# A linear-attention and MLP block on one core: a head with fewer constant matmuls, a written ScalarE order, and four row norms on GpSimd

## The chip, the cores and the metric

The kernel runs on one core of a Trainium2 chip. A core has a matrix engine (TensorE, PE in the profile, with its weight loads as PEld), a vector engine (VectorE, DVE), a scalar engine (ScalarE, ACT), GpSimd (POOL) and SyncE (SP), which here only issues DMAs. The metric is the device time of one execution in microseconds; lower is better.

## The reference

`x` is 1 x 2048 x 448 in bfloat16. It is normalised row by row (mean and variance over the 448 columns, no scale or shift), and two branches read the result.

```
xn = layernorm(x)
q, k, v = split(xn @ wqkv)            # 16 heads of 28
pq, pk = phi(q), phi(k)               # phi(t) = t + 1 where t > 0, else exp(t); + 1e-6
kv = sum_s pk[s] v[s]^T ;  z = sum_s pk[s]        # per head
s  = ((pq @ kv) / (pq . z + 1e-6)) @ wo
h  = relu(xn @ w1 + b1)^2             # 1792 columns
g  = silu(h @ w2 + b2)
out = x + s * g
```

## The kernel before

**Tiles.** The 2048 rows are 16 tiles of 128 rows (`si`), in four groups of four (`g`). The 448 columns are contracted in chunks of 128, 128, 128 and 64; the last 64 columns use half the array, so the kernel pairs two matmuls on the two halves. The 1792 hidden columns are 14 slots (`fi`). Results go through eight PSUM banks.

**A planner sets the order.** The program is first a list of operations. `add` (L54) records one: its engine, what it reads and writes, and a duration that the author wrote down. TensorE and SyncE keep the order of the program text. For ScalarE, VectorE and GpSimd, `one_pass` (L98) plays the list through with those written durations and picks, whenever an engine is free, the most urgent ready operation by its due time or by a fixed `prio`; some operations may float between ScalarE and VectorE. It also hands out the banks. `behind` holds an operation until another has been placed, and `at` overrides when the planner believes a DMA lands. The chip then runs each engine's list strictly in that order, with semaphores for the dependences. So a changed duration or landing time can move operations that the edit does not name.

**The head, tiles 0 to 3.** For each tile: two statistics instructions on VectorE (`bn`, `ag`, L490 and L491), ln and exp on ScalarE for the reciprocal deviation (`ln`, `rs`, L498 and L502), the norm on VectorE (`xn`, L520), transposes on TensorE (`T`, L597), and their evacuation to `xT` (`eT`, L606 and L607, most on ScalarE). The last 64 columns of a pair of tiles are copied beside themselves by a twin copy (`tw`, L536 or L537), transposed together (`TR`, L621) and evacuated (`eTR`, L631). TensorE then does the K projection of tiles 0 and 1 (`K0`, `K1`, L795) and two hidden slots (`Ha0`, `Ha1`, L823, on tiles 0 and 1 as `.0` and on tiles 2 and 3 as `.2`), with a small transpose of the bias between them (`B1`, L1228). Ahead of and between these stand matmuls on a zeroed tile `dum` (`warm`, L1213): 30 at once, 9 that wait for the statistics of tile 0, and 6 between T0 and T1.

**The body.** TensorE goes through the hidden slots of group 0 in pairs (`H0.2` to `H0.13`, L780), then `K2|K3`, then the second MLP product (`G`, L1086) of tiles 0 to 3, each `G` in parts over the slots: G0|G1, G2|G3, then the second half of G0|G1, which reads the squares of the later slots, and so on. Then it takes up group 1 with `H1.0`. Each `H` result is a bank that ScalarE or VectorE turns into `relu` (`re`, L758 or L755), and two slots at a time are squared (`sq`, L770 or L769). Each `K` is turned into phi by an exp on ScalarE (`ex`, L701) and a min and a max on VectorE (`mi`, L706, and `ma`, L713); the max frees the bank.

**Tiles 4 to 7** do not go through TensorE's transpose. Their norms are written interleaved, two tiles alternating by column (`xn_cols`); VectorE copies the twins (`tw4`, `tw6`) and transposes 32 x 32 blocks as 32-bit words into `stage` (`tr4`, `tr6`, L557), and 16 DMAs (13 issued by SyncE, 3 by ScalarE, each of 32 KB) put the blocks into `xT`. H1.0 waits for all of them. Tiles 8 to 15 follow the same way later, with `gbuf` in the place of `stage`.

**GpSimd** writes masks and constants until 7.3 us (L371 to L415) and, when w_q has landed, one small scaled copy (`wqh`, L1278). Before the kernel's own code the framework writes four small constants on GpSimd (L1380 in the profile), among them a bfloat16 1.0.

Of the kernel before, what the change touches and what calls it, by code (L numbers as in the profile page):

```python
# [9 lines left out]
P = 128  # L10
# [12 lines left out]
SWAP = 1  # L23
# [23 lines left out]
class Program:  # L47
# [6 lines left out]
    def add(self, eng, emit, reads=(), writes=(), dur=0.2, alts=(), nbytes=0, mode=None, label="", slow=1.0):  # L54
        op = Op(eng, emit, reads, writes, dur, alts, nbytes, mode, label)
        op.slow, op.behind, op.at = slow, None, None
        for t in op.reads:
            op.raw.add(self.writer[t])
            self.readers.setdefault(t, []).append(op)
        for t in op.writes:  # L60
            w = self.writer.get(t)
            if w is not None and w is not op:
                op.deps.add(w)
            for r in self.readers.get(t, ()):
                if r is not op:
                    op.deps.add(r)
            self.writer[t] = op
            self.readers[t] = [r for r in self.readers.get(t, ()) if r is op]
        op.raw.discard(op)
        op.deps |= op.raw  # L70
        for d in op.deps:
            d.succ.append(op)
        self.ops.append(op)
        return op
# [233 lines left out]
def bass_recurrent_scan__linear_attn_block__dense_activation_squared_relu__prompt_kernel(  # L308
    nc, A_x, A_wqkv, A_wo, B_x, B_w1, B_b1, B_w2, B_b2, out
):  # L310
    with ExitStack() as es:
        sb = lambda name, shape, dtype: es.enter_context(nc.sbuf_tensor(name, shape, dtype))
        bf, f32 = dt.bfloat16, dt.float32
        pr = Program()
        add = pr.add

        ident = sb("ident", [P, P], bf)
        dum = sb("dum", [P, P], bf)
# [8 lines left out]
        xn = sb("xn", [P, NT, 512], bf)  # L327
# [8 lines left out]
        b1r = sb("b1r", [NF, P], bf)  # L336
        b1f = sb("b1f", [P, NF], f32)
        b2b = sb("b2b", [P, D], bf)
        st6 = sb("st6", [P, NT, 6], f32)
        mv = sb("mv", [P, NT, 2], f32)  # L340
        vep = sb("vep", [P, NT], f32)
        rstd = sb("rstd", [P, NT], f32)
# [18 lines left out]
        ps = lambda b: pbank[b.bank]  # L361
# [124 lines left out]
        def hp(si, k):  # L486
            return None if si > 3 else 5 * si + k - 25
# [18 lines left out]
        def xn_cols(si, lo, hi):  # L506
            if si < 4 * SWAP:
                return xn[:, si, lo:hi]
            pair_of = xn[:, si // 2 * 2 : si // 2 * 2 + 2, :].rearrange("p t f -> p (t f)")
            return pair_of.rearrange("p (f t) -> p f t", t=2)[:, lo:hi, si % 2]  # L510
# [4 lines left out]
            return v.rearrange("p (j k t) -> p j k t", j=2, t=2)[:, si % 4 // 2, :, si % 2]  # L515

        def ln_norm(si):
            add(
                "dve",
                lambda e, _: e.tensor_scalar(  # L520
                    out=xn_cols(si, 0, D), in0=x_tok[:, si, :], scalar1=mv[:, si, 0:1],
                    scalar2=rstd[:, si : si + 1], op0=ALU.subtract, op1=ALU.mult,
                ),
                [("x", si), ("mv", si), ("rstd", si)], [("xn", si)], 0.39 if si < 4 * SWAP else 0.54, label=f"xn{si}",
            ).prio = hp(si, 3)

        def ln_twin(lo, hi):
# [61 lines left out]
        def pe_transpose(si, pieces):  # L589
            for lo, hi, eng in pieces:  # L590
                b = Buf("T")

                def f(e, _, lo=lo, hi=hi, b=b):
                    v = ps(b)[:, :].bitcast(bf)
                    last = None
                    for c in range(lo, hi):
                        last = e.transpose(v[:, (c - lo) * P : (c - lo + 1) * P], xn[:, si, c * P : (c + 1) * P], ident[:, :])  # L597
                    return last

                add("pe", f, [("xn", si), "ident"], [b], 0.0558 * (hi - lo), mode="128", label=f"T{si}.{lo}")  # L600

                def ev(e, eng, lo=lo, hi=hi, b=b):
                    src = ps(b)[:, 0 : 64 * (hi - lo)].bitcast(bf)
                    dst = xT[:, si, lo:hi, :].rearrange("p c k -> p (c k)")
                    if eng == "dve":
                        return e.tensor_copy(dst, src)  # L606
                    return e.activation(out=dst, in_=src, func=AF.Copy)  # L607

                n = hi - lo
                add(  # L610
                    eng, ev, [b], [("xT", si, c) for c in range(lo, hi)],
                    0.15 + 0.07 * n if eng == "dve" else 0.18 + 0.107 * n, label=f"eT{si}.{lo}",
                ).prio = -30
# [590 lines left out]
            return b, reads, mm, out_, D, f"S{si}", 4  # L1204


        def warm(n, after=()):
            b = Buf("W")

            def f(e, _):  # L1210
                last = None
                for _i in range(n):
                    last = e.matmul(ps(b)[:, 0:P], dum[:, 0:P], dum[:, 0:P], start=True, stop=True)  # L1213
                return last

            add("pe", f, ["dum", *after], [b], n * 0.075, mode="128", label="warm")

        for i in range(4):
            ln_stats(i)
            ln_rstd(i, i + 1)  # L1220
            ln_norm(i)
            if i % 2:
                ln_twin(i - 1, i + 1)

        def bias_cols():
# [4 lines left out]
            )  # L1230
            add("act", lambda e, _: e.activation(out=b1f[:, :], in_=ps(bb)[:, 0 : NF // 2].bitcast(bf), func=AF.Copy), [bb], ["b1f"], 0.2, label="b1f")

        warm(30)
        warm(9, [("mv", 0)])
        pe_transpose(0, ((0, 3, "act"),))
        warm(6)
        pe_transpose(1, ((0, 3, "act"),))
        k_part(0, 0, 3)
        pe_transpose_rests(0)
        k_part(1, 0, 3)  # L1240
        head_part(0, 0)
        pe_transpose(2, ((0, 3, "act"),))
        head_part(0, 1)
        bias_cols()
# [4 lines left out]
        head_part(2, 1)  # L1249
        head_rest(0)  # L1250

        order = "bn0 ag0 bn1 ag1 xn0 xn1 bn2 ag2 bn3 ag3 xn2 xn3".split()
        byname = {op.label: op for op in pr.ops}
        for a, b in zip(order, order[1:]):
            byname[b].behind = byname[a]
            byname[b].prio = -25 + order.index(b)
        landing = {("x", 0): 2.9, ("x", 1): 3.55, ("x", 2): 4.7, ("wk", 0): 5.8, ("wk", 3): 5.0, ("wk", 4): 5.4, ("w10", 0): 7.0, ("w10", 3): 7.2, ("w10", 4): 7.4, ("b1r", None): 7.6, ("w11", 0): 9.7, ("w11", 3): 10.0, ("w11", 4): 10.3, ("x", 4): 11.4}
        for (name, k), t in landing.items():
            byname["dma" + str((name, k) if k is not None else name)].at = t

        def ln(lo, hi):
            for si in range(lo, hi):
                ln_stats(si)
            ln_rstd(lo, hi)
            for si in range(lo, hi):
                ln_norm(si)
            ln_twin(lo, hi)
# [86 lines left out]
        a, b = "G10|G11", "G12|G13"  # L1354
# [40 lines left out]
```

## Time and profile before

| | us |
|---|---|
| median of 3 runs | 143.94 (143.91 to 144.25) |
| the profiled execution | 143.42 |
| its span, first to last instruction | 142.2 |
| TensorE busy | 138.6 |
| VectorE busy | 103.2 |
| ScalarE busy | 78.9 |
| GpSimd busy | 6.2 |

Times in the profile run from the start of the span. The 1.2 us between the span and the execution's time lie outside the instructions, and the median of the runs is 0.52 us above the profiled execution. A row of the timeline has start, length, engine, line, operation, output and inputs, count, and in brackets the engine's idle time ahead of it with what ended it. A row of the chain has start, length, engine and line of the work that led to the end.

### The profile page before, as it was taken

The numbers are of one execution on the slowest core, as the hardware profiler recorded it, in microseconds if no ns is written. First come the engines' busy times: TensorE is split into PE (matmuls) and PEld (weight loads), VectorE is DVE, ScalarE is ACT, GpSimd is POOL, SyncE is SP. The second block draws the span as 40 slices with busy tenths as digits, with TensorE's granted clock in tenths as the row PEclk, the third lists the DMA queues.
The fourth block names the chain that finished last, engine by engine and source line by source line (L and its number), as shares of the span: only waits on it lengthen the run. The fifth ranks groups of instructions, "written<-read, shape, count | busy, mean of one in ns | idle before, by whom it ended". The sixth has DMA issues, their size and how long they took to land.

```text
span 142.2 us, 3235 instructions
## 1 busy us (share of the span) xinstructions
PE 138.6 (97%) x1300; PEld 71.7 (50%) x1300; DVE 103.2 (73%) x222; ACT 78.9 (55%) x146; POOL 6.2 (4%) x40
## 2 busy tenths in 40 slices
PE   7999999999999999999999999999999999999992
PEld 7954445454444544444544444445547455555472
DVE  2847999689498899769787799786035516874875
ACT  3578898040888724997863757797139430301412
POOL 7900000000000000000000000000000000000000
PEclk9999999999999999999999999999999999999999
DMA  4999994238933000232000000000697000223033
GB/s 97 319 306 311 344 271 72 34 53 254 227 44 55 14 0 0 46 53 44 9 5 0 0 0 5 0 0 19 156 214 155 1 0 22 93 83 101 32 97 97
DMA packets 23500, 12.91 MB, mean 91 GB/s; under 512 B 14274, under 2 KB 22718, under 8 KB 23486
## 3 DMA queue, kind: packets, MB, share of 16 engines
q1 hardware_dynamic: 21550, 11.24, 31.5%
q10 hardware_dynamic: 1936, 1.48, 4.3%
q8 instruction: 10, 0.16, 0.5%
q14 instruction: 4, 0.03, 0.1%
HBM read 9.23 MB, written 1.90 MB: 78 GB/s over the span
## 4 chain that ended last, share of the span: by engine, by line
PE 97%; DVE 2%; issue 0%
PE pb L780 29%; PE pb L1086 22%; PE pb L1178 7%; PE pb L881 7%; PE pb L723 7%; PE pb L733 6%; PE pb L1103 4%; PE pb L1213 4%; PE pb L1143 3%; PE pb L860 1%; DVE gbuf L1167 1%; PE pb L887 1%; PE pb L823 1%; PE pb L795 1%; PE pb L1030 1%; PE pb L597 1%
## 5 line engine op out<-in xcount | busy, mean ns | idle before, releaser
L780 PE MATMUL pb<-xT,w 64*128 64x512 bf16 x378 | 43.6, 376 | 0.0
L1086 PE MATMUL pb<-w,r 64*128 64x448 bf16 x336 | 34.6, 349 | 0.0
L758 ACT ACTIVATE r<-pb,b1f 128x512 bf16<-128x512 f32 x40 | 25.7, 686 | 12.9 <-PE pb L780 12.4
L780 PEld LDWEIGHTS pb<-xT,w 64*128 64x128 bf16 x378 | 18.4, 94 | 21.7
L1086 PEld LDWEIGHTS pb<-w,r 64*128 64x128 bf16 x336 | 16.3, 94 | 15.9 <-issue 0.4
L770 ACT ACTIVATE r<-r 128x1024 bf16<-128x1024 bf16 x15 | 15.7, 1062 | 0.6 <-DVE r L755 0.5
L755 DVE TENSOR_SCALAR r<-pb,b1f 128x512 bf16<-128x512 f32 x16 | 11.7, 744 | 4.5 <-PE pb L780 4.5
L1198 DVE TENSOR_TENSOR gbuf<-pb,gbuf 128x448 bf16<-128x448 f32 x14 | 8.1, 618 | 6.6 <-PE pb L1178 6.6
L490 DVE BATCH_NORM_STATS2 st<-x_tok 128x6 f32<-128x448 bf16 x16 | 9.5, 615 | 2.9 <-DMA x_tok<-in_A_x_dram 2.9
L723 PE MATMUL pb<-w_k,xT 64*128 64x448 bf16 x98 | 11.6, 349 | 0.0
L733 PE MATMUL pb<-xT,w_q 64*128 64x512 bf16 x84 | 11.0, 376 | 0.0
L1126 ACT ACTIVATE gbuf<-gbuf 128x448 bf16<-128x448 bf16 x14 | 7.0, 570 | 6.7 <-DVE gbuf L1076 5.9
L1178 PE MATMUL pb<-w_k,pqT 64*128 64x448 bf16 x96 | 10.6, 349 | 0.0
L1076 DVE TENSOR_TENSOR gbuf<-pb,b2b 128x448 bf16<-128x448 f32 x14 | 8.0, 614 | 3.4 <-PE pb L1086 2.0
L713 DVE SCALAR_TENSOR_TENSOR pk<-pb,pk 128x448 bf16<-128x448 f32 x16 | 9.5, 617 | 0.2
L994 DVE TENSOR_TENSOR pqT<-pqT,xT 128x2048 bf16<-128x2048 bf16 x3 | 3.7, 1221 | 8.2 <-DMA xT<-scr 8.2
L701 ACT ACTIVATE pqT<-pb 128x512 bf16<-128x512 f32 x12 | 6.5, 597 | 5.6 <-PE pb L733 5.6
L881 PE MATMUL pb<-pk,xn 128*128 128x448 bf16 x48 | 9.6, 353 | 0.0
L701 ACT ACTIVATE pk<-pb 128x448 bf16<-128x448 f32 x16 | 7.8, 543 | 3.1 <-PE pb L723 2.5
L769 DVE TENSOR_TENSOR r<-r 128x1024 bf16<-128x1024 bf16 x13 | 8.5, 682 | 0.1
L917 DVE TENSOR_TENSOR zacc<-zacc,pk 128x448 f32<-128x448 f32 x13 | 8.0, 618 | 0.1
L520 DVE TENSOR_SCALAR xn<-x_tok,mv,rstd 128x448 bf16<-128x448 bf16 x16 | 7.4, 498 | 0.8 <-ACT rstd L502 0.7
(98 smaller groups left out, 134.6 us busy)
## 6 DMA issues: line engine op xcount, KB each, us to landing
w<-in_B_w_dram SPq DMA_DIRECT2D x1, 1568.0 KB, 10.3
out_dram<-gbuf SPq DMA_DIRECT2D x13, 112.0 KB, 1.7
x_tok<-in_A_x_dram SPq DMA_DIRECT2D x3, 448.0 KB, 5.7
xT<-gbuf SPq DMA_DIRECT2D x32, 32.0 KB, 2.0
w<-in_B_w_dram SPq DMA_DIRECT2D x2, 384.0 KB, 5.9
xT<-scr SPq DMA_DIRECT2D x6, 112.0 KB
w<-in_B_w_dram SPq DMA_DIRECT2D x1, 576.0 KB, 5.5
xT<-scr ACTq DMA_DIRECT2D x5, 112.0 KB
```

The source lines that it names most:

```text
L490: add("dve", lambda e, _: e.bn_stats(st6[:, si, :], x_tok[:, si, :]), [("x", si)], [("st", si)], 0.61, label=f"bn{si}").prio = hp(si, 0)
L701: "act", lambda e, _: e.activation(out=slot, in_=ps(buf)[0:rows, 0:n], func=AF.Exp), [buf, "actw"],
L713: lambda e, _: e.scalar_tensor_tensor(out=slot, in0=ps(buf)[0:rows, 0:n], scalar=1.0 + 1e-6, in1=slot, op0=ALU.add, op1=ALU.max),
L723: return e.matmul(ps(b)[:, 0:D], x_tile(rows, si, c), w_k[rows, c, :], start=start, stop=stop)
L733: return e.matmul(ps(b)[:, 0:512], w_q[rows, c, m * P : (m + 1) * P], x_group(rows, g, c), start=start, stop=stop,)
L755: return e.tensor_scalar(out=slot, in0=ps(b)[:, 0:512], scalar1=b1f[:, fi : fi + 1], scalar2=0.0, op0=ALU.add, op1=ALU.max)
L758: return e.activation(out=slot, in_=ps(b)[:, 0:512], func=AF.Relu, bias=b1f[:, fi : fi + 1])
L770: return e.activation(out=both, in_=both, func=AF.Square)
L780: return e.matmul(ps(b)[:, 0:512], w_1[rows, c, fi * P : (fi + 1) * P], x_group(rows, g, c), start=start, stop=stop,)
L881: last = e.matmul(ps(b)[:, 0:D], xn_cols(si, c * P, (c + 1) * P), pk[:, si, :], start=(si == 0), stop=(si == NT - 1),)
L1086: return e.matmul(ps(b)[:, 0:D], r_cols(rows, fi, si), w_2[rows, fi, :], start=start, stop=stop)
L1178: return e.matmul(ps(b)[:, 0:D], w, msb[rows, c, :], start=start, stop=stop)
```

## The change

Four edits, and what follows from them:

- `warm` can take an operand of its own and then waits for nothing. Three warm-up matmuls on the framework's constant 1.0, seen as a 128 x 128 tile, are put first; of those on `dum`, 9 become 8 and 6 become 3. The planner is told 0.107 us for each instead of 0.075, and for the transposes of tiles 0 and 1 0.107 instead of 0.0558.
- The order of ScalarE's work in the head is written out and held with `behind` and `prio`, as VectorE's already was.
- The norms of tiles 4 to 7 go to GpSimd, with 0.85 us written for each.
- The landing times that the planner is told (`landing`, set through `at`) are replaced.
- The plan that comes out differs in places that no edit names: VectorE and ScalarE trade some relus and squares in groups 0 to 2, the banks are numbered otherwise, and tw4 and tw6 wait for GpSimd. SyncE's list is the same, and so are the lists of all engines from the denominators to the end.

```diff
         def ln_norm(si):
+            by_pool = 4 <= si < 8
             add(
-                "dve",
+                "pool" if by_pool else "dve",
...
-                [("x", si), ("mv", si), ("rstd", si)], [("xn", si)], 0.39 if si < 4 * SWAP else 0.54, label=f"xn{si}",
+                [("x", si), ("mv", si), ("rstd", si)], [("xn", si)], 0.39 if si < 4 * SWAP else 0.85 if by_pool else 0.54, label=f"xn{si}",
             ).prio = hp(si, 3)
...
-                add("pe", f, [("xn", si), "ident"], [b], 0.0558 * (hi - lo), mode="128", label=f"T{si}.{lo}")
+                add("pe", f, [("xn", si), "ident"], [b], (0.107 if si < 2 else 0.0558) * (hi - lo), mode="128", label=f"T{si}.{lo}")
...
-        def warm(n, after=()):
+        one = nc.const_aps.tensor(1.0, [P, P], bf)
+
+        def warm(n, after=(), src=None):
             b = Buf("W")
...
-                    last = e.matmul(ps(b)[:, 0:P], dum[:, 0:P], dum[:, 0:P], start=True, stop=True)
+                    last = e.matmul(ps(b)[:, 0:P], src or dum[:, 0:P], src or dum[:, 0:P], start=True, stop=True)
                 return last
 
-            add("pe", f, ["dum", *after], [b], n * 0.075, mode="128", label="warm")
+            add("pe", f, ["dum", *after] if src is None else [], [b], n * 0.107, mode="128", label="warm")
...
+        warm(3, src=one)
         warm(30)
-        warm(9, [("mv", 0)])
+        warm(8, [("mv", 0)])
         pe_transpose(0, ((0, 3, "act"),))
-        warm(6)
+        warm(3)
         pe_transpose(1, ((0, 3, "act"),))
...
-        order = "bn0 ag0 bn1 ag1 xn0 xn1 bn2 ag2 bn3 ag3 xn2 xn3".split()
         byname = {op.label: op for op in pr.ops}
-        for a, b in zip(order, order[1:]):
-            byname[b].behind = byname[a]
-            byname[b].prio = -25 + order.index(b)
...
+        for first, order in (
+            (-26, "bn0 ag0 bn1 ag1 xn0 xn1 bn2 ag2 bn3 ag3 xn2 xn3"),
+            (-61, "rs1 eT0.0 tw0 eT1.0 ln2 rs2 ln3 rs3 eTR0 eT2.0 b1f"),
+        ):
+            names = order.split()
+            for i, (a, b) in enumerate(zip(names, names[1:])):
+                byname[b].behind = byname[a]
+                byname[b].prio = first + 1 + i
+            if first < -26:
+                byname[names[0]].prio = first
```

More of the change, by code (lines that the diff above doesn't have):

```diff
@@ L1250, in bass_recurrent_scan__linear_attn_block__dense_activation_squared_relu__prompt_kernel @@
         head_rest(0)
-        order = "bn0 ag0 bn1 ag1 xn0 xn1 bn2 ag2 bn3 ag3 xn2 xn3".split()
         byname = {op.label: op for op in pr.ops}
-        for a, b in zip(order, order[1:]):
-            byname[b].behind = byname[a]
-            byname[b].prio = -25 + order.index(b)
-        landing = {("x", 0): 2.9, ("x", 1): 3.55, ("x", 2): 4.7, ("wk", 0): 5.8, ("wk", 3): 5.0, ("wk", 4): 5.4, ("w10", 0): 7.0, ("w10", 3): 7.2, ("w10", 4): 7.4, ("b1r", None): 7.6, ("w11", 0): 9.7, ("w11", 3): 10.0, ("w11", 4): 10.3, ("x", 4): 11.4}
+        for first, order in (
[8 more added lines that the diff above has]
+                byname[names[0]].prio = first
+        landing = {("x", 0): 2.92, ("x", 1): 3.9, ("x", 2): 4.65, ("wk", 0): 5.7, ("wk", 3): 5.7, ("wk", 4): 7.2, ("w10", 0): 6.97, ("w10", 3): 7.2, ("w10", 4): 7.4, ("b1r", None): 7.5, ("w11", 0): 9.1, ("w11", 3): 9.4, ("w11", 4): 9.8, ("x", 4): 11.3}
         for (name, k), t in landing.items():
```

## The prediction

> **What bounds the kernel now.** I read the page's busy shares, then the chain of waits in order of time, then the timeline of the first 36 us, then the GpSimd groups.
>
> ```profile
> PE 138.6 (97%) x1300; PEld 71.7 (50%) x1300; DVE 103.2 (73%) x222; ACT 78.9 (55%) x146; POOL 6.2 (4%) x40
> ...
> PE 97%; DVE 2%; issue 0%
> ```
>
> TensorE holds 97% of the chain, so the rest of the kernel matters only where TensorE waits for it. The chain shows where that can be:
>
> ```profile
> 1.06 4.34 PE pb L1213 x39
> 5.40 0.32 PE pb L597 x3
> 5.72 0.64 PE pb L1213 x6
> 6.36 0.32 PE pb L597 x3
> 6.68 0.84 PE pb L795 x3
> 7.63 0.57 PE pb L795 x3
> ...
> 11.11 9.06 PE pb L780 x84
> ...
> 22.82 2.65 PE pb L1086 x28
> ```
>
> From 11.11 on the steps run at one pace: 84 matmuls of 512 columns in 9.06 us are 0.216 us a pair, 28 of 448 columns in 2.65 us are 0.189 us a pair, and the same shapes cost the same up to the tail. There is nothing to win there, only something to lose. The first 11 us are different: six warm-up matmuls take 0.64 us (0.107 us each), the transposes also 0.107 us each, and three K matmuls first take 0.84 us and then 0.57 us. So the array runs at about half pace until roughly 7.1 us, although the page's PEclk row shows 9 throughout; I take the pace from the spacing.
>
> The timeline gives the waits around the change:
>
> ```profile
> 5.76 0.49 ACT L607 ACTIVATE xT<-pb 128x384 bf16<-128x384 bf16 x1 [0.39 <-PE pb L597]
> ...
> 8.12 0.22 PEld L823 LDWEIGHTS pb<-xT,w 128*128 128x128 bf16 x3 [0.37 <-DMA w<-in_B_w_dram]
> ...
> 9.95 0.55 PEld L823 LDWEIGHTS pb<-xT,w 128*128 128x128 bf16 x6 [0.31 <-DVE xT L606]
> ...
> 12.44 1.15 DVE L490 BATCH_NORM_STATS2 st<-x_tok 128x6 f32<-128x448 bf16 x2 [0.80 <-DMA x_tok<-in_A_x_dram]
> ...
> 19.21 0.96 DVE L520 TENSOR_SCALAR xn<-x_tok,mv,rstd 128x448 bf16<-128x448 bf16 x2
> ...
> 20.44 0.71 DVE L557 STREAM_TRANSPOSE stage<-xn 128x512 f32<-128x512 f32 x1
> 21.07 0.71 DVE L755 TENSOR_SCALAR r<-pb,b1f 128x512 bf16<-128x512 f32 x1
> 21.18 9.76 SPq L429 DMA_DIRECT2D xT<-stage  x13
> ...
> 22.66 2.81 PE L1086 MATMUL pb<-w,r 64*128 64x448 bf16 x28
> ...
> 33.25 0.29 PEld L780 LDWEIGHTS pb<-xT,w 64*128 64x128 bf16 x4
> ```
>
> At 8.12 the first w_1 matmul (Ha0.0) waits for its weights from HBM, not for work that the change shortens. At 9.95 Ha0.2 waits for VectorE's evacuation eT3. The rows from 19.21 to 21.18 are the chain that prepares tiles 4 to 7: norms, twin copy, transpose (tr6), 13 DMAs on SyncE's queue. The last two are its consumers: at 22.66 G2|G3, then G0|G1's second half, and at 33.25 the first weights of H1.0.
>
> ```profile
> L397 POOL TENSOR_SCALAR_AFFINE_SELECT zmask<-zmask 128x32 f32<-128x32 f32 x12 | 2.2, 216 | 0.0
> L373 POOL TENSOR_SCALAR_AFFINE_SELECT ident<-ident 128x128 bf16<-128x128 bf16 x1 | 0.3, 292 | 0.2 <-POOL eps L379 0.2
> L1278 POOL TENSOR_SCALAR wqh<-w_q 128x64 bf16<-128x64 bf16 x1 | 0.2, 242 | 14.2 <-DMA w_q<-in_A_wqkv_dram 14.2
> ```
>
> GpSimd has one TENSOR_SCALAR, of 64 columns, and is otherwise idle after 7.3 us.
>
> **The constant matmuls.** The first three need no `dum`, whose memset ends at 1.00 us, so TensorE can begin near 0.85 (ScalarE's first instruction starts at 0.80) instead of 1.06: -0.21. Ahead of T0 stand 41 instead of 39: +0.21. T0 stays at 5.2. Behind it stand 3 instead of 6: 3 x 0.107 = -0.32. T1 would start at 5.83 instead of 6.15, but xn1 ends at 5.41 + 0.40 = 5.81, so near 5.87. K0 then waits for eT0, which ends at 5.76 + 0.49 = 6.25: it starts near 6.33 instead of 6.47, so 0.14 is left. Half pace lasts for 0.14 us more of K0's work, which gives back about 0.07. K1 ended at 8.03 (7.46 plus three times 0.19); it would end at 7.96, and Ha0.0 still starts at 8.12 when its weights land. In this execution the gain is 0; if the weights land 0.3 us earlier it is up to 0.19. I take 0.05, near the end that the row shows.
>
> **ScalarE's written order.** In the changed program ScalarE's first 25 instructions, through rs4, stand as before; the list pins those of the head. With T1 earlier, eT1 ends 0.25 earlier, and with it ln2, rs2 and xn2 (7.66, which waited 0.38 for rstd). T2 reads xn2 but stands behind Ha0.0 on TensorE, and T3, eT3 and Ha0.2 stand behind those: 0.
>
> **Norms 4 to 7.** VectorE loses four norms at about 0.48 us spacing (0.96 a pair). That hides behind TensorE: 0. GpSimd gets them behind the last constants (done at 7.3) and ahead of wqh, which needs w_q at 21.4 anyway. What is new is that VectorE's twin copies tw4 and tw6 wait for GpSimd. The new plan puts behind tw6: tr6, all three last squares of group 0 (one was on ScalarE), the statistics of tile 8, and K2/K3's phi. SyncE's 13 DMAs wait for tr6, and the second half of G0|G1 on TensorE waits for the squares.
>
> I add up starts on VectorE by the rows' spacing: statistics of 4 and 5 at 12.44 (x lands); +1.29; K1's min and max +0.85 (now behind the statistics); two relus +0.66 each; square +0.61; statistics of 6 and 7 +1.28: 17.79. ScalarE: square 4.5 waits for relu 0.4 until 15.98, +1.0, two relus +0.57 each, ln and exp +0.53: rstd 6 at 18.7. GpSimd runs xn6 and xn7 from 18.75 to 18.75 + 2p. VectorE is free for tw6 at about 20.1.
>
> The price p of one norm, from both sides: from 32 to 128 columns the select goes from 216 to 292 ns, 0.79 ns a column, so wqh's 242 + 384 x 0.79 = 0.55 us at 448. If all of wqh's 242 ns grew with the columns, it would be 242 x 448/64 = 1.69 us. VectorE's own norm goes from 0.40 to 0.53 where the output is interleaved; that ratio on 0.55 gives 0.74. I take 0.74: the slope is GpSimd's own, and the output here is interleaved. Then tw6 starts at 20.3, tr6 ends at 21.24 (before: 21.15), and the third square ends 2.73 us after tw6, at 23.0. G0|G1's second half starts at 22.66 + 14 x 0.0946 = 23.98 and loads weights about 0.15 sooner: 0.8 us of cover. The last staged DMA landed at about 32.3 (issued 30.33, 2.0 to land); H1.0 loads weights at 33.25: 0.9 us of cover. Both are used up at p = 1.15. Below that the cost is 0.
>
> **Another new wait.** H0.8 takes the bank that K1's max frees. That ends now at 12.44 + 1.29 + 0.31 + 0.59 = 14.63 instead of 14.32, and TensorE reaches it at about 14.65: 0 here, and at most 0.1 when the head runs early. It also ties TensorE to x of tile 4 at 12.42, so a gain over 0.1 in the head is lost again here unless that lands earlier too.
>
> **The sum.** The tail's orders are unchanged. 143.42 us (span 142.2 and 1.2 around it) - 0.05 = 143.37. The median of the runs is 0.52 above that execution; I carry the offset: 143.94 - 0.05 = 143.89, rounded to 143.9.
>
> **Rivals.** (1) GpSimd becomes the bound, slower: p over 1.15, and each further 0.1 costs 0.2 us on G0|G1, since two norms stand in series. At 1.5 that is +0.70 (144.6), at the bound of 1.69 +1.08 (145.0). For it: no row has GpSimd at 448 columns, an interleaved output or per-partition scalars. Against it: wqh, the same operation, lies on the line of the other GpSimd rows. VectorE's square 6.7 (18.62 to 19.3) also falls on xn6. In the rows ten selects ran in 1.80 us from 4.41, 0.18 each, across VectorE's xn0 and xn1, so sharing cost little. [...]
>
> (2) The clock, faster: pace doubles near 7.1, 6.0 us after the first matmul. If an earlier start moves that ahead of 6.1, K0 and K1 take 0.57 each from 6.1 and Ha0.0 could start at 7.4 instead of 8.12: up to 0.7 us (143.2) if the w_1 weights are there, 0 if they land at 8.1. [...]
>
> **Chances.** Forecast, all hidden, 143.7 to 144.0: 0.57. GpSimd slow enough to show (p over about 1.4), 0.25. Clock and weights both early, 0.18. A measurement of this kernel can tell about 0.3% (0.43 us) from no change. Range 143.4 to 144.6: it takes in p up to 1.5 and the smaller half of the clock's gain, and leaves out about 0.1 on each side. Faster 0.18, same 0.57, slower 0.25.
>
> **What would show it.** Right: Ha0.0 still waiting for DMA near 8.1; GpSimd's four norms under 1.1 us each; VectorE idle little before tw6; the first L1086 group in one pace. Wrong: a gap in TensorE near 24 or 33 released by VectorE or by DMA, or the first K matmuls already at 0.19 us spacing.

## The result, and the profile after

The changed kernel takes 145.14 us (median of 7 runs, 144.33 to 145.37) against 143.97 for the kernel before on the same chip (143.47 to 144.25): a ratio of 1.0066 with a 95% interval of 1.0038 to 1.0093. It is slower, by 0.7%, and by what the first rival described. The profiled execution took 144.82 us with a span of 143.6, 1.4 longer than the span before.

On the page the three lines to compare are the busy times, the shares of the chain and a group that was not there before.

```profile
PE 138.7 (97%) x1299; PEld 71.4 (50%) x1299; DVE 103.6 (72%) x221; ACT 75.9 (53%) x143; POOL 14.0 (10%) x44
...
PE 80%; DVE 6%; DMA 4%; SPq 4%; POOL 3%; ACT 2%; issue 1%
...
L521 POOL TENSOR_SCALAR xn<-x_tok,mv,rstd 128x448 bf16<-128x448 bf16 x4 | 7.9, 1993 | 7.5 <-ACT rstd L502 7.5
```

TensorE is as busy as before, but it holds 80% of the chain instead of 97%: the chain now runs through other engines for a fifth of the time. The last line has the reason: one GpSimd norm takes 1993 ns, where the forecast took 740 and thought 1690 the most it could be.

The chain shows where that meets TensorE (start, length, what):

```profile
18.33 0.21 ACT rstd L502
...
18.63 3.94 POOL xn L521 x2
...
22.59 0.21 DVE xn L537
...
22.83 0.71 DVE stage L558
23.54 1.79 DVE r L770 x3
...
25.37 1.50 PE pb L1087 x14
```

Read downwards it is the path that the prediction followed: reciprocal deviations of tiles 6 and 7, their two norms in series, the twin copy tw6, the transpose tr6, the three squares, and then G0|G1's second half on TensorE. The weight loads of that half say how long TensorE stood (idle time ahead, and its releaser):

```profile
25.37 1.06 PEld L1087 LDWEIGHTS pb<-w,r 64*128 64x128 bf16 x14 [1.78 <-DVE r L770]
```

These loads run ahead of their matmuls (at G2|G3 they began at 22.35 and the matmuls at 22.54); by the spacing of the matmuls themselves the gap is 1.51 us, and it is the only long one that the trace before does not have. Up to K0 the head went as forecast: T1 starts at 5.79 instead of 6.15 and K0 at 6.26 instead of 6.47, and then

```profile
8.01 0.50 PE L824 MATMUL pb<-xT,w 128*128 128x256 bf16 x3 [0.18 <-DMA w<-in_B_w_dram]
```

the first w_1 matmul still waits for its weights from HBM, which landed 0.11 us earlier in this execution than in the one before. 1.51 - 0.11 = 1.40 is the difference of the spans.

### The profile page after: what moved, and what is told of

Same layout as the page of the kernel before. It is cut to its first block, busy times and chain, and to the rows that moved or that the text cites. A ratio compares the mean times of both kernels' runs of the same rounds, so it can differ in the third digit from the quotient of the medians.

```text
span 143.6 us, 3234 instructions
## 1 busy us (share of the span) xinstructions
PE 138.7 (97%) x1299; PEld 71.4 (50%) x1299; DVE 103.6 (72%) x221; ACT 75.9 (53%) x143; POOL 14.0 (10%) x44
## 4 chain that ended last, share of the span: by engine, by line
PE 80%; DVE 6%; DMA 4%; SPq 4%; POOL 3%; ACT 2%; issue 1%
PE pb L781 22%; PE pb L1087 20%; PE pb L1179 7%; PE pb L882 6%; PE pb L734 6%; PE pb L724 6%; DMA x_tok<-in_A_x_dram 4%; SPq L429 4%; PE pb L1104 4%; PE pb L1144 3%; POOL xn L521 3%; PE pb L861 1%; DVE r L770 1%; DVE gbuf L1168 1%; PE pb L888 1%; PE pb L1031 1%
## 5 line engine op out<-in xcount | busy, mean ns | idle before, releaser
L1087 PE MATMUL pb<-w,r 64*128 64x448 bf16 x336 | 34.7, 349 | 1.3 <-DVE r L770 1.3
L1087 PEld LDWEIGHTS pb<-w,r 64*128 64x128 bf16 x336 | 16.2, 94 | 17.5 <-DVE r L770 1.8
L771 ACT ACTIVATE r<-r 128x1024 bf16<-128x1024 bf16 x12 | 12.6, 1059 | 0.5 <-DVE r L756 0.4
L770 DVE TENSOR_TENSOR r<-r 128x1024 bf16<-128x1024 bf16 x16 | 10.4, 682 | 0.1
L521 POOL TENSOR_SCALAR xn<-x_tok,mv,rstd 128x448 bf16<-128x448 bf16 x4 | 7.9, 1993 | 7.5 <-ACT rstd L502 7.5
```

The source lines that it names most:

```text
L521: lambda e, _: e.tensor_scalar(out=xn_cols(si, 0, D), in0=x_tok[:, si, :], scalar1=mv[:, si, 0:1], scalar2=rstd[:, si : si + 1], op0=ALU.s ...
L770: return e.tensor_tensor(out=both, in0=both, in1=both, op=ALU.mult)
L771: return e.activation(out=both, in_=both, func=AF.Square)
L1087: return e.matmul(ps(b)[:, 0:D], r_cols(rows, fi, si), w_2[rows, fi, :], start=start, stop=stop)
```

## The experiments

Two theories stood at the start. **A**: the price of a GpSimd norm, two in series, holds up G0|G1's second half, and the rest of the change neither gains nor loses. **B**: the rearranged plan (ScalarE's order, landing times, banks) costs the time, and the GpSimd norms only stand beside it. Each result below has its own ratio to the kernel before, measured on the same chip beside it; where only one run was taken, there is no ratio.

### Taking the change apart

**The norms back on VectorE** (`by_pool = False` in the changed kernel).

> The changed kernel with the norms of tiles 4 to 7 back on VectorE; the constant matmuls, ScalarE's written order and the landing times stay. Theory A (two GpSimd norms of 1.99 us in series hold tw6, tr6 and the squares, and that alone cost the time): the 1.5 us gap ahead of G0|G1's second half near 23.7 is gone, Ha0.0 still waits for its w_1 weights and starts near 8.0, and the median is within 0.3 us of the kernel before: 143.7 to 144.1. Rival B (the written ScalarE order, the replaced landing times and the renumbered banks cost it, and the GpSimd norms only stand beside): most of the +1.2 stays, 144.8 to 145.3. Rival C (the head edit has a gain that the GpSimd stall covered): 0.3 to 0.4 us under the kernel before, 143.5 to 143.7.

Measured: 143.57 us (143.26 to 144.95, 12 runs), ratio 1.0011 (0.9985 to 1.0036). Everything but the norms is worth nothing that can be measured. B falls, and so does C, a hidden gain of the head: the median lies in C's range, but on this chip the kernel before took 143.66, and the two are equal. Its profiled execution was one whose loads came late, and shows among others these two waits:

```profile
8.35 0.50 PE L824 MATMUL pb<-xT,w 128*128 128x256 bf16 x3 [0.60 <-DMA w<-in_B_w_dram]
...
15.91 1.47 PE L781 MATMUL pb<-xT,w 64*128 64x512 bf16 x11 [0.36 <-DVE pk L714]
```

The first is the wait of the head. The second is the bank wait of H0.8 on K1's max: x of tile 4 came at 13.66 instead of 12.44, and the max stands behind its statistics.

**The norms alone** (the kernel before, with `by_pool = 4 <= si < 8` and 0.85 us written).

> The kernel before with one edit: the norms of tiles 4 to 7 on GpSimd, planned at 0.85 us. Head, landing times and ScalarE's order are those of before. Theory A: a pair of norms takes 3.9 to 4.0 us, tw6 starts near 22.6 to 22.8, TensorE stands 1.5 to 1.7 us ahead of G0|G1's second half, and the median is 1.2 to 1.7 us above the kernel before: 145.2 to 145.7. Rival B: no gap there, 143.9 to 144.2.

Measured: 145.19 us (144.95 to 145.91, 5 runs), ratio 1.0119 (1.0090 to 1.0148). The four norms took 1.98 to 2.03 us each, the gap ahead of G0|G1's second half is 1.51 us. The norms alone make a loss of the size of the gap. It is larger than that of the whole change (1.0066), but the two were measured on different chips and their intervals touch; whether the rest of the change gives a little back can't be told.

**The planner told the true price** (`0.85` becomes `2.0` in the changed kernel).

> The changed kernel, but the planner is told 2.0 us for a GpSimd norm instead of 0.85. Its plan puts the squares of group 0 ahead of tw6 and tr6 on VectorE, so G0|G1's second half no longer waits for GpSimd. Theory A as it stands (the norms' lateness itself must be paid somewhere): xn7 still ends near 22.6, so the 16 staged DMAs still start near 23.5 and land near 34.1, as in the changed kernel; TensorE now reaches H1.0 at about 33.2 and waits there 0.9 to 1.1 us for DMA instead: 144.5 to 145.0. Rival D (only the wrong written duration cost the time, by the order that it made): the stall is gone altogether, 143.7 to 144.1.

Measured: 145.04 us (144.22 to 145.79, 6 runs), ratio 1.0100 (1.0065 to 1.0135). The order that the planner makes of the true number is no better. The profiled execution, the fastest of the six, has no gap at G0|G1's second half, and its chain ends elsewhere:

```profile
18.70 4.53 POOL xn L521 x2
...
32.20 1.95 DMA xT<-stage
...
34.20 1.90 PE pb L781 x15
```

The norms end at 23.2, 0.6 later than in the changed kernel: the new order puts squares on VectorE ahead of tw6, and xn7 took 2.49 us instead of 1.99. The transpose and its 13 DMAs on SyncE's queue follow, and TensorE waits for the last of them at H1.0 (0.35 us in this execution, less than expected; it had lost 0.47 ahead of the first G before). D falls by the median. In this execution the lateness moved from one consumer of the norms to the other; what the slower ones lost beyond that, no trace shows.

**One GpSimd norm instead of four** (`by_pool = si == 7`).

> The changed kernel with only the norm of tile 7 on GpSimd; tiles 4 to 6 are back on VectorE. A GpSimd norm still takes 2.0 us. Theory A (what counts is when the pair 6, 7 is done, two norms in series being 3.9 us against the 2.3 that the cover allows): one norm of 2.0 stays inside the cover, so no gap ahead of G0|G1's second half, 143.5 to 143.8 (as with no norm on GpSimd). [...]

Measured: 144.31 us (143.82 to 145.17, 12 runs), ratio 1.0049 (1.0025 to 1.0072). This missed: it is over the range of A and inside that of a rival, E: any work of GpSimd beside VectorE on these tiles costs, VectorE's instructions between 14 and 23 us get longer, and about half the loss stays (144.2 to 144.5). The run alone did not tell why. In the profiled execution, its fastest, the one norm took 2.25 us, beside a VectorE norm:

```profile
19.06 2.25 POOL L521 TENSOR_SCALAR xn<-x_tok,mv,rstd 128x448 bf16<-128x448 bf16 x1 [11.72 <-ACT rstd L502]
```

So GpSimd's instruction got longer there, while VectorE's norm beside it kept its 0.53. No gap came of it: w_2 landed at 20.97 and made TensorE wait 0.57 us ahead of the first G. But VectorE's last square ended at 24.19, just as TensorE loaded weights for it at 24.30, so nothing was left of the cover. What the slower executions lost, no trace here shows, so E is not refuted by this run.

### The price of a GpSimd norm

**Ten forms late in the kernel, where nobody waits for GpSimd.**

> The kernel before, with 20 extra GpSimd instructions from about 36 us on, whose output nothing reads: ten forms, two of each. They price the norm of GpSimd: (0) the norm as changed, two per-partition scalars, interleaved output, 448 columns; (1) the same with contiguous output; (2) two immediate scalars, interleaved; (3) two immediate scalars, contiguous; (4, 5) as 3 with 224 and 64 columns; (6, 7) as 1 with 224 and 64 columns; (8) a plain copy, contiguous; (9) a plain copy, interleaved. If the interleaved output is the price, 0 takes 2.0 and 1 about half. If it is the per-partition scalars, 0 and 1 take 2.0, and 2 and 3 take 0.6 to 0.8. If it is a price by column in every form, 3 takes 1.7 (242 ns for 64 columns, scaled), and 4 half of that. [...]

```profile
L1296 POOL TENSOR_SCALAR pr<-x_tok,mv,rstd 128x448 bf16<-128x448 bf16 x2 | 4.1, 2033 | 0.2
L1295 POOL TENSOR_SCALAR pr<-x_tok,mv,rstd 128x448 bf16<-128x448 bf16 x2 | 4.0, 1990 | 11.8 <-DMA x_tok<-in_A_x_dram 11.7
...
L1298 POOL TENSOR_SCALAR pr<-x_tok 128x448 bf16<-128x448 bf16 x2 | 1.1, 564 | 0.2
```

L1295 is the norm with its interleaved output, L1296 the same with contiguous output, L1298 two multiplications by immediate scalars. The layout is not the price. The form that wqh has takes 564 ns at 448 columns: the prediction's estimate from the selects' slope, 0.55, was right for that form. Both the kind of scalar and the operation differ between the dear and the cheap rows, so these forms do not say which it is. The time is 143.72 us (10 runs), ratio 1.0007 (0.9986 to 1.0028), where 143.9 to 144.2 had been expected if that work cost VectorE nothing: 20 us of GpSimd work that nobody waits for cost nothing that can be measured.

**Scalars or operation.** The same place, six forms.

> The kernel before, with 18 extra GpSimd instructions from about 35 us on, whose output nothing reads: six forms of one 448-column contiguous instruction, three of each. (0) subtract and multiply with two per-partition scalars, (1) the same with two immediate scalars, (2) the first scalar per partition and the second immediate, (3) the other way round, (4) multiply and multiply with two per-partition scalars, (5) one subtraction with one per-partition scalar. In the forms run before, two per-partition scalars took 1.86 us at least and two immediate ones 0.56, but the operations differed too. If reading a per-partition scalar is the price, 0 and 4 take 1.9, 1 takes 0.56, and 2, 3 and 5 take 1.2 where each scalar costs by itself, or 1.9 where one is enough. If the subtraction is the price, 0, 1, 2, 3 and 5 take 1.9 and 4 takes 0.56.

```profile
L1296 POOL TENSOR_SCALAR pr<-x_tok,mv,rstd 128x448 bf16<-128x448 bf16 x3 | 5.6, 1860 | 12.8 <-DMA x_tok<-in_A_x_dram 12.6
...
L1297 POOL TENSOR_SCALAR pr<-x_tok 128x448 bf16<-128x448 bf16 x3 | 5.2, 1722 | 0.3
L1301 POOL TENSOR_SCALAR pr<-x_tok,mv 128x448 bf16<-128x448 bf16 x3 | 4.6, 1525 | 0.3
L1300 POOL TENSOR_SCALAR pr<-x_tok,mv,rstd 128x448 bf16<-128x448 bf16 x3 | 2.3, 755 | 0.3
```

L1296 is subtract and multiply with two per-partition scalars, L1297 the same with immediate ones, L1301 one subtraction alone, L1300 multiply and multiply with two per-partition scalars. The subtraction is the price: with immediates it still takes 1.72, and without it two per-partition scalars take 0.755 (0.72 at the least). The two forms with one scalar of each kind, which also subtract, took 1.79 to 1.91. One run: 143.72 us.

**Is it subtraction, or anything but multiplication?**

> The kernel before, with 15 extra GpSimd instructions from about 35 us on, whose output nothing reads: five forms of 448 columns, three of each, all with two per-partition scalars: (0) multiply then add, interleaved output, (1) multiply then add, contiguous, (2) add then multiply, contiguous, (3) multiply then subtract, contiguous, (4) multiply then multiply, interleaved. The runs before showed 1.86 us for subtract then multiply and 0.72 for multiply then multiply, both contiguous. If it is the subtraction alone, 0, 1, 2 take 0.7 to 1.0 and only 3 takes 1.8. If only multiply by multiply is fast, 0 to 3 all take 1.7 to 2.0 and 4 takes 0.9 to 1.1 (0.72 and the 0.14 to 0.54 by which the interleaved form with immediate scalars was longer).

```profile
L1299 POOL TENSOR_SCALAR pr<-x_tok,rstd,mv 128x448 bf16<-128x448 bf16 x3 | 6.8, 2261 | 0.3
...
L1296 POOL TENSOR_SCALAR pr<-x_tok,rstd,mv 128x448 bf16<-128x448 bf16 x3 | 2.5, 843 | 12.8 <-DMA x_tok<-in_A_x_dram 12.6
...
L1297 POOL TENSOR_SCALAR pr<-x_tok,rstd,mv 128x448 bf16<-128x448 bf16 x3 | 2.4, 800 | 0.3
```

Multiply then subtract (L1299) takes 2.26 us; multiply then add takes 0.80 contiguous (L1297) and 0.84 interleaved (L1296). Add then multiply took 0.71 to 1.02, and multiply then multiply, interleaved, 0.85 to 1.20. It is the subtraction alone. One run: 143.09 us.

### The price put back into the kernel

**The same program with a cheap instruction** (`op0=ALU.subtract` becomes `op0=ALU.mult` for tiles 4 to 7).

> The changed kernel with one word changed: in the four GpSimd norms the subtraction of the mean is a multiplication, so that the mean is left out of the norm of tiles 4 to 7. Every engine's order is that of the changed kernel; only the price of the GpSimd instruction differs. Theory A (the price of the subtraction, two in series, is the whole loss): the four take 0.9 to 1.1 us each, the pair 6, 7 ends near 20.8 instead of 22.6, the gap ahead of G0|G1's second half falls from 1.5 to 0 to 0.2 us, and the median is 143.5 to 143.9. [...]

```profile
L521 POOL TENSOR_SCALAR xn<-x_tok,mv,rstd 128x448 bf16<-128x448 bf16 x4 | 3.7, 956 | 10.2 <-ACT rstd L502 10.2
```

The gap ahead of G0|G1's second half is gone from the trace; all orders are those of the changed kernel. Measured: 144.09 us (143.33 to 144.59, 12 runs), ratio 1.0005 (0.9980 to 1.0031): no loss that can be measured against the kernel before, with a median above the range that A expected and below the 144.4 from which on E, a cost of GpSimd's work in any form, was to show. That median and the run with one norm left a question: does GpSimd's work cost anything besides the gap?

### The loads out of the way

One number taken from the traces settles where the executions differ: the span less the start of the first G (the first L1086 or L1087 matmul of the timeline). The span is read to 0.1 us, so the last column holds within 0.05.

| kernel | first G, us | from there to the end |
|---|---|---|
| before | 20.77 | 121.43 |
| changed | 20.65 | 122.95 |
| norms back on VectorE | 21.86 | 121.44 |
| norms alone on GpSimd | 20.97 | 122.93 |
| planner told 2.0 | 21.15 | 121.85 |
| one GpSimd norm | 21.11 | 121.49 |
| multiply for subtract | 21.38 | 121.42 |

Where GpSimd is not in the way, the rest takes 121.4 to 121.5 us, whatever the kernel. In the changed kernel and with the norms alone it takes 1.5 more, which is the gap, and with the planner told 2.0 about 0.4 more, the wait at H1.0. With one norm or with cheap ones it takes nothing more: what those two executions lost, they lost before the first G, and there w_1, x of tile 4 and w_2 land at other times in each execution: in these seven traces Ha0.0 started at 7.72 to 8.35 and the statistics of tile 4 at 12.35 to 13.66, and w_2 took 10.3 us from issue to landing in the kernel before and 11.35 with one GpSimd norm. The kernels that follow take these waits away.

```diff
-load_main("sp", w_1, B_w1, "w10", cuts[0], cuts[1])
+load_main("sp", w_1, B_w1, "w10", 0, 2 * P)         # slots 0 and 1 first
...
+load_main("sp", w_1, B_w1, "w13", 2 * P, 4 * P)     # after b1r
...
-dma("sp", w_2[:, :, :], ...)
+dma("sp", w_2[:, 0:7, :], ...)                      # G's first part reads only these
+dma("sp", w_2[:, 7:14, :], ...)
...
+named["bn4"].behind = named["maK1"]
```

> The changed kernel with all norms on VectorE and three edits that take waits for HBM off TensorE: the first w_1 load is cut in two (the slots of Ha0 and Ha1 first), w_2's load is cut in two (slots 0 to 6 first), and the statistics of tile 4 stand behind K1's max on VectorE, so that H0.8 no longer waits for x of tile 4. Theory A (the head edit gains nothing because Ha0.0 waits for HBM): Ha0.0 starts near 7.7 instead of 8.0 to 8.35, the first G has its half of w_2 in time (its wait was 0 to 0.5 us by execution), H0.8 does not wait: 0.3 to 0.8 us under the kernel before, 142.9 to 143.4. Rival F (the loads are bound by bandwidth, and what lands earlier makes the rest later by as much): a new wait at H0.2 or at the later slots of w_1 takes it back, 143.5 to 143.8.

Measured: 143.19 us (142.86 to 144.42, 12 runs), ratio 0.9983 (0.9957 to 1.0009).

> The kernel before with the same three edits to the loads and to the statistics of tile 4, and nothing of the change. It tells what the changed head is worth once the weights are early. If the head edit is worth its 0.2 to 0.36 us there, this kernel is that much slower than the one with the changed head: 143.2 to 143.6. If the clock's release, which came at 5.9 us in one execution of this head and at 7.1 in another, sets when K1 ends, or the loads still do, the two are equal within 0.15.

Measured: 143.01 us (142.65 to 144.37, 12 runs), ratio 0.9965 (0.9937 to 0.9993). In both traces no matmul from Ha0.0 to the first G waits for a DMA, and the first G starts at 20.30 and 20.45; nothing in them speaks for F. The two medians are 0.18 apart, the changed head being no faster; both kernels have three executions of twelve above 144.2, and no trace shows those. The last edit did nothing yet, since the planner put tile 5's statistics, which need the same load, in the freed place.

The next kernel holds both (`bn4` and `bn5`), and loads x of tiles 4 to 7 in two halves:

> The kernel before with the loads of w_1 and w_2 cut in two as in the two runs before, x of tiles 4 to 7 loaded in two halves, and the statistics of both tiles 4 and 5 held behind K1's max (in the runs before, the planner put those of tile 5 in the freed place, so H0.8 still hung on x). Theory A: the median of 143.0 stays or falls a little, 142.7 to 143.0, and the executions near 144.3 (3 of 12), if they are late landings of x, are gone. Rival F (bandwidth): the extra load delays the later ones, 143.1 to 143.4, and the late executions stay.

Measured: **142.99 us (142.76 to 143.15, 7 runs), ratio 0.9928 (0.9902 to 0.9954)**. This is the version that beats both the kernel before and the change. The times near 144.3 did not come back in its seven runs, which is too few to say that they are gone.

> The same edits on the changed kernel with all norms on VectorE, so that the two differ in the head alone. With no load in TensorE's way, the changed head is worth what it gains up to Ha0.0: 0.15 us by the profiles of the two runs before (H0.2 at 10.64 against 10.79), 0.2 to 0.36 by its own matmuls. Theory A: 0.1 to 0.3 us under its partner, 142.5 to 142.8. Rival: equal within 0.1, because the clock's release or a landing sets the end of the head.

Measured: 143.04 us (142.68 to 144.16, 12 runs), ratio 0.9961 (0.9933 to 0.9988). The changed head is equal to the old one within what can be measured, even here. Two of the twelve executions took 144.02 and 144.16, so with these loads late executions still come. In the two traces Ha0.0 starts at 7.37 with the changed head and at 7.80 with the old one, but in the latter K0 stood 0.45 us for w_k's load: with w_1 early, the head hung on another landing in that execution.

**The last two** are this kernel with GpSimd's norms as the change writes them, and with the norm as multiply and add:

```diff
+nbias[:, si] = (mv[:, si, 0] * rstd[:, si]) * -1.0          # GpSimd, one column
-xn = (x - mv) * rstd
+xn = x * rstd + nbias
```

> The kernel before with the cut loads of w_1, w_2 and x and the statistics of tiles 4 and 5 behind K1's max, and with the norms of tiles 4 to 7 on GpSimd as the change writes them (subtract, then multiply). Here no load should cover or blur the stall: TensorE reaches G0|G1's second half near 23.8, and two norms of 1.9 to 2.0 in series still end near 22.3 to 22.6, the third square near 25. Theory A: a gap of 1.1 to 1.6 us there, and a median 1.1 to 1.6 above the same kernel with VectorE's norms (142.99): 144.1 to 144.6. If the loss in the runs with one GpSimd norm and with the cheap norms (144.31 and 144.09, each 0.3 to 0.5 above what was expected) came from a cost of GpSimd's work that is not this gap, it is more: 144.9 or above.

```profile
14.41 8.33 POOL xn L525 x4
...
23.00 0.71 DVE stage L562
23.71 1.79 DVE r L774 x3
...
25.55 1.50 PE pb L1091 x14
```

Measured: 144.84 us (144.56 to 145.14, 6 runs), ratio 1.0074 (1.0050 to 1.0098). The gap is 1.80 us, and the median lies 144.84 - 142.99 = 1.85 above the kernel with VectorE's norms (1.70 if one counts that the kernel before took 143.91 beside this one and 143.76 beside that one): the gap accounts for the loss. From the first G to the end it takes 123.28 us, 1.8 more than without. The gap is longer than expected because the first two norms, with a square on VectorE beside the first, took longer: tw4 started 4.47 us after their start, and 3.97 in the changed kernel. The second two took 3.9 again, and the series from 14.41 ended at 22.74; TensorE stood ready at 25.55 - 1.80 = 23.75, as expected.

> The same, but GpSimd's norm computes x times rstd plus a second per-partition number, minus mean times rstd, which one more GpSimd instruction of one column a tile prepares. The result is the whole norm. Multiply then add took 0.84 us with the interleaved output against 1.99 for subtract then multiply. Theory A (the instruction's form is the whole loss): a pair takes 2.0 us with the two small ones at most, tw6 starts near 20.7, there is no gap ahead of G0|G1's second half, and the median is that of the kernel with VectorE's norms: 142.8 to 143.2. Rival E (GpSimd on this path costs in any form, or x's landing decides): 0.3 us or more above it, 143.3 to 143.6.

Measured: 143.25 us (142.80 to 144.33, 12 runs), ratio 0.9962 (0.9938 to 0.9985), against 0.9928 (0.9902 to 0.9954) with VectorE's norms: the intervals overlap. The median lies between the ranges of A and E. The profiled execution is the slowest of the twelve (144.33):

```profile
12.40 0.55 PEld L805 LDWEIGHTS pb<-xT,w 64*128 64x128 bf16 x8 [1.50 <-DMA w<-in_B_w_dram]
...
18.93 0.87 POOL L528 TENSOR_SCALAR nbias<-mv,rstd 128x1 f32<-128x1 f32 x2 [1.05 <-ACT rstd L506]
19.79 1.62 POOL L536 TENSOR_SCALAR xn<-x_tok,rstd,nbias 128x448 bf16<-128x448 bf16 x2
```

The pair of norms is done 2.5 us after the deviations instead of 3.9, and nothing waits for it: from the first G to the end it takes 121.43 us. What this execution lost is a wait of 1.2 us, by the matmuls' spacing, for a load of w_1 that landed near 12.36. So without the subtraction GpSimd's norms cost nothing that shows in a trace. Whether they cost up to the 0.26 us between the two medians can't be told from these runs. The late load leaves rival F open: cutting the loads did not make their landings steady (this one landed near 12.36 here, and in the trace with VectorE's norms H0.2 to H0.13 ran from 10.61 without a wait), and no run shows whether bandwidth is the reason.

## Why the prediction was wrong, step by step

**The price p of one GpSimd norm: the step that failed.** It was bounded from wqh and the selects, 0.55 to 1.69 us, taken as 0.74, and measured 1.99 in the changed kernel. The slope gave 0.55, and the form it came from takes 0.56; the widening for the interleaved output was of the right kind (0.80 to 0.84 for multiply and add). What failed is the sentence that wqh is "the same operation": it has the same name in the profile and the same instruction, but multiplies twice, and the norm subtracts. No row of the trace before had a GpSimd subtraction, so the upper end was no bound at all. "No row has GpSimd at 448 columns, an interleaved output or per-partition scalars" listed three differences, and the one that mattered was a fourth.

**The mechanism: right.** The break point of 1.15 us and 0.2 us for each further 0.1 give 2 x (1.99 - 1.15) = 1.68 us at the measured price; the gap is 1.51. The parts fit: the deviations were ready for xn6 at 18.63 (predicted 18.75), and the third square ended 23.54 + 1.79 - 22.59 = 2.74 us after tw6 began (predicted 2.73). The second cover, at H1.0, was not called on, since TensorE came 1.5 us later there; with the planner told 2.0 it was. That the rival's time at its bound, 145.0, came so near the measured 145.14 is in part luck: at the measured price its rule gives 143.89 + 1.68 = 145.57. The medians differ by 1.17, less than the gap in the trace, and what made up the rest is not shown.

**The constant matmuls: right in the result.** K1 ended earlier, and Ha0.0 waited for HBM. How much earlier was wrong: K1's last matmul began at 7.48 and so ended near 7.67, not 7.96, because the pace doubled in K0 already, near 6.6 us instead of 7.1; the wait for the weights hid it. It did so in nine of the ten traces with the old loads, whichever head they had, and started at 7.7 to 8.35. The head alone is worth nothing (ratio 1.0011). "Up to 0.19 if the weights land earlier" does not show in the medians either: with the weights early, 143.04 stands against 142.99.

**ScalarE's order: right**, as far as the same run shows; it was not tried by itself.

**H0.8's bank wait on K1's max: mis-sized.** Taken as 0 to 0.1 us. In the changed kernel's trace it is 0, but with the old loads the statistics of tile 4 started at 12.35 to 13.66 us, and at 13.66 the matmuls stood 0.53 us. The kernel before has the same tie.

**The clock, the other rival: the pace moved, and with the old loads that gained nothing.** That the clock sets the pace was the author's reading: the page's PEclk row shows 9 throughout, before and after, and no trace shows what makes the pace double. By the spacing of the matmuls (on the constant tile 0.107 us, then 0.056) the pace doubled near 7.1 us in the profiled execution before, at 5.7 with the ten forms and near 4.1 with the norms alone, all three with the old head. In the last of these K1's last matmul began at 7.04, and Ha0.0 still waited for its weights until 8.00; with the ten forms it waited until 8.17. So the forecast of nothing gained "if they land at 8.1" held. With the loads cut, an early doubling may count: with the changed head the pace doubled near 6.6 in one execution and near 5.2 in another, and Ha0.0 started at 7.67 and 7.37.

**GpSimd beside VectorE: not what failed.** The prediction took from ten selects beside VectorE's norms that working side by side costs little. In the changed kernel a norm took 1.99 us beside a whole square of 0.65 and 1.99 beside nothing, so the step did not fail by this. In other runs GpSimd's instructions did get longer beside VectorE's: see the last section.

## What to carry to other kernels

Before work is moved to another engine, its price has to come from a row with the same arithmetic on that engine, not only the same instruction name; where there is none, the upper bound is open, and one run with a few idle instructions of the exact form settles it. On GpSimd, write a norm as multiply and add (0.84 us here, interleaved), not as subtract and multiply (1.99). And where a head waits for loads, cut the load so that its first consumer's part lands first, before shortening the work ahead of it: here the kernel before with the cut loads and tile 4's statistics moved took 0.9965 of its time, and the shorter head with the old loads 1.0011.

## What the runs showed of the hardware

- GpSimd's tensor-scalar instruction at 448 bfloat16 columns: 0.56 us for two multiplications by immediates; with two per-partition scalars 0.72 at the least for multiply and multiply and 0.71 for multiply and add; 1.40 to 1.77 for one subtraction, 1.71 to 2.49 for subtract and multiply, 1.96 to 2.46 for multiply then subtract.
- One column was not cheap there: the four products for `nbias` took 0.46 us on the mean, with squares on VectorE beside part of them, and the 64 columns of wqh 0.24.
- Beside VectorE, GpSimd's instructions got longer in some overlaps and not in others. wqh took 0.72 us in the execution with the ten forms and 0.24 in that with the six; with squares on VectorE beside all of it, it took 0.41 with the norms as multiply and add, and kept 0.24 with multiply for subtract. In that last run a norm took 1.30 beside 0.57 of a square, and 0.84 to 0.85 where at most 0.27 fell on it. A subtracting norm took 2.25 instead of 1.99 beside a VectorE norm of 0.53, and 2.49 with the planner told 2.0. But in the changed kernel neither the norm (1.99) nor the square inside it (0.65) got longer.
- VectorE's last three squares of group 0 took 1.93 us with wqh beside them, in the run with multiply for subtract, and 1.85 in the changed kernel, where wqh ran ahead of them.
- The pace of TensorE doubled near 4.1 us in one execution (the norms alone) and near 7.1 in another (the kernel before), with the same instructions ahead and the first matmul at 1.04 and 1.06.
